# Agent attention and an MLP on one core: 128-row key subtiles, 512-token tiles, half as many native pairs, another queue order

## The chip, the core and the metric

The kernel runs on one core of a Trainium2 chip. The core has five engines with a queue each: TensorE (PE in the rows, with PEld its weight loads) makes matrix products into PSUM, VectorE (DVE), ScalarE (ACT) and GpSimd (POOL) work elementwise, and SyncE (SP) starts the transfers between HBM and SBUF. Each engine runs its own queue in order; semaphores make one wait for another. The metric is the device time in microseconds (us) of one execution; lower is better.

## What is computed

```python
def attn(q, k, v, agents):            # q, k, v [2, 12480, 128], agents [2, 49, 128]
    scale = 1.0 / np.sqrt(q.shape[-1])
    def sm(a, b):
        s = scale * (a @ b.transpose(0, 2, 1))
        e = np.exp(s - s.max(-1, keepdims=True))
        return e / (e.sum(-1, keepdims=True) + 1e-09)
    agent_v = sm(agents, k) @ v       # 49 agents look at all keys of their batch
    return sm(q, agents) @ agent_v    # each query looks at the 49 agents

def moe(x, w_in, w_out):              # x [24960, 128], w_in [128, 2048], w_out [2048, 128]
    h = x @ w_in
    g = np.where(h >= 1, h, np.where(h <= -1, 0.0, (h + 1) ** 2 / 4))
    return g @ w_out
```

The second function is applied to the result of the first, for all 2 x 12,480 tokens. The MLP's weights arrive as float64.

## The kernel before

The program has a start, in which the first batch's agent values are made, and a main loop over output tiles.

*Start.* The keys of batch 0 are loaded in 13 groups of 8 subtiles of 120 tokens (`kbuf`, four buffers, L419). For each subtile TensorE multiplies the keys, 120 columns of them as the stationary side, by the agents of both batches, 98 columns (`scores`, L442; a float32 product is two records of two passes each). ScalarE copies the scores to `ks`, VectorE keeps a running maximum, GpSimd subtracts it, and ScalarE takes the exponential. Then v is loaded in 13 groups of 8 subtiles (`vbuf`, four buffers, L542), and TensorE multiplies `ks` (stationary, 49 columns) by v with a column of ones beside it, 129 columns (`av`, L560). The ones give the softmax's sum. The sums of all groups (`acc`, L576), divided, are multiplied into w_in (`weights`, L624), so that the query's attention and the first MLP product become one product per tile. w_in and w_out are put together from their float64 words by VectorE and GpSimd (`decode`, L314 to L349).

*Main loop.* 52 tiles of 480 tokens. For each, `queries` scores four subtiles of 120 queries against the 49 agents (L660), takes a softmax (L673 to L708: maximum, difference, exponential, sum, an addition of 1e-9 at L692, reciprocal, product, and a split into a rounded high part and a rest), transposes it (L716) and copies it to `mt`, 98 rows of high and low parts. `pair` then takes 256 of the 2,048 hidden columns at a time, eight pairs a tile: four products into a PSUM pair `ph` (L755, w_hi and w_lo for two chunks; three such pairs exist), two ScalarE steps (`relu` L764, `square` L769) and a VectorE step (`gate` L772, which frees `ph`) that make g, then a high part `ghi` (`hi`, on VectorE L259 or ScalarE L257) and a low part `glo` (`lo` L783, on GpSimd or VectorE), and six products into the tile's accumulator bank (L793: ghi with w_out's high and low parts, glo with its high part). I call these six and the four ahead of them split products. In a native pair (N in `HI_ENG`) ghi and glo are left out and two float32 products take g as it is, four records of two passes each. `output` copies the bank (`ot`) and stores it.

*Batch 1's keys and values* go through the same steps during the main loop, with scores of 49 columns (the group's 120 rows by one batch's agents) in a free accumulator bank. Two of its key groups (16 subtiles) stand ahead of the first MLP product on TensorE.

*What sets the order.* `Order` (a planner inside the kernel) places each small operation by rough durations and by keys, the urgencies in `KEYS0`, `KEYS1`, `START` and `NEXT`; it fixes every engine's queue, and the order in which SyncE issues the transfers. Where `HI_ENG` or `LO_ENG` leaves a choice, it picks the engine too. The durations have no other effect.

## Time and profile before

| | |
|---|---|
| median of 3 runs | 1127.57 us (1126.28 to 1129.03) |
| the profiled execution: its span | 1129.6 us |
| TensorE busy | 1104.9 us, 98% |
| VectorE busy | 985.3 us, 87% |
| ScalarE busy | 961.0 us, 85% |
| GpSimd busy | 649.4 us, 57% |
| first MLP product begins | 86.6 us |
| transfers | 56.36 MB |

The profile is of one execution, and its span of 1129.6 us, from the first instruction to the last, is that execution's own time; it lies 2.0 us above the median. Busy time of TensorE counts products that overlap one another, so a full TensorE says little by itself; the distance from one product's start to the next one's tells what a product costs. The elementwise engines' records also reach some 0.1 us into the next one's.

### The profile page before, as it was taken

To read this page: it belongs to the slowest core of one execution; us is meant where nothing else is said; L and a number is where in the kernel's file an instruction comes from. 1 tells how busy PE (TensorE), PEld (TensorE's weight loads), DVE (VectorE), ACT (ScalarE), POOL (GpSimd) and SP (SyncE) were. 2 spreads that over 40 slices of the span, in tenths; PEclk is the share of its full clock that TensorE was granted. 3 is DMA by queue.
4 is the path that set the end of the run, shared out by engine and by line. 5 is a ranking of instruction groups with operands and counts; after the bars stand their busy time and mean duration, and the time that the engine had idled before them with its cause. 6 is when DMAs were issued, how large, how long until landed. Compare 5 with 4: busy or idle time off the path is not lost.

```text
span 1129.6 us, 15421 instructions
## 1 busy us (share of the span) xinstructions
PE 1104.9 (98%) x5546; PEld 919.5 (81%) x5546; DVE 985.3 (87%) x1310; ACT 961.0 (85%) x1155; POOL 649.4 (57%) x356
## 2 busy tenths in 40 slices
PE   9779999999999999999999999999999999999998
PEld 8657888888877888888887888888888888888886
DVE  7559998988897787888888999899999999999987
ACT  3219988989998888887898999999999999999997
POOL 2425756655676665555565565656565656565654
PEclk9889999999999999999999999999999999999999
DMA  8995111100002221200100101010101010100000
GB/s 302 205 257 121 53 53 38 51 18 27 20 25 53 62 62 45 62 18 18 36 19 20 34 18 35 18 36 19 36 18 35 18 36 18 36 10 18 10 18 18
DMA packets 47122, 56.36 MB, mean 50 GB/s; under 512 B 2758, under 2 KB 43334, under 8 KB 47046
## 3 DMA queue, kind: packets, MB, share of 16 engines
q1 hardware_dynamic: 47046, 55.37, 17.9%
q8 instruction: 44, 0.72, 0.3%
q14 instruction: 32, 0.26, 0.1%
HBM read 42.58 MB, written 12.78 MB: 49 GB/s over the span
## 4 chain that ended last, share of the span: by engine, by line
PE 91%; DMA 3%; ACT 2%; DVE 2%; SPq 1%; POOL 1%; issue 1%; DVEq 0%; ACTq 0%; POOLq 0%
PE bank L793 48%; PE ph L755 31%; PE bank L660 3%; PE bank L560 2%; PE ph L442 2%; PE bank L442 1%; PE bank L716 1%; DMA vbuf<-v_in 1%; ACT g L764 1%; DMA qt<-qT 1%; PE ph L560 1%; DVE g L772 1%; DMA kbuf<-kT 1%; POOL glo L783 1%; SPq L542 1%
## 5 line engine op out<-in xcount | busy, mean ns | idle before, releaser
L783 POOL TENSOR_TENSOR glo<-g,ghi 128x960 fp32r<-128x960 f32 x208 | 539.3, 2596 | 373.4 <-DVE ghi L259 298.5
L772 DVE SCALAR_TENSOR_TENSOR g<-g,ph 128x960 f32<-128x960 f32 x416 | 473.3, 1148 | 70.2 <-ACT g L769 39.4
L764 ACT ACTIVATE g<-ph,half 128x960 f32<-128x960 f32 x416 | 438.5, 1059 | 79.6 <-PE ph L755 56.9
L769 ACT ACTIVATE g<-g 128x960 f32<-128x960 f32 x416 | 414.4, 1004 | 5.2
L755 PE MATMUL ph<-mt,w_hi 98*128 98x480 f32 x832 | 334.7, 402 | 2.1 <-DVE g L772 2.1
L755 PE MATMUL ph<-mt,w_lo 98*128 98x480 f32 x832 | 315.1, 379 | 0.0
L793 PE MATMUL bank<-glo,wo_hi 128*128 128x480 f32 x728 | 225.0, 393 | 0.0
L793 PE MATMUL bank<-ghi,wo_hi 128*128 128x480 f32 x728 | 223.1, 387 | 0.9 <-ACT ghi L257 0.9
L793 PE MATMUL bank<-ghi,wo_lo 128*128 128x480 f32 x728 | 217.8, 380 | 0.0
L259 DVE CAST ghi<-g 128x960 fp32r<-128x960 f32 x312 | 207.0, 688 | 0.5
L783 DVE TENSOR_TENSOR glo<-g,ghi 128x960 fp32r<-128x960 f32 x156 | 183.3, 1180 | 6.4 <-ACT ghi L257 6.4
L755 PEld LDWEIGHTS ph<-mt,w_hi 98*128 98x128 f32 x832 | 156.4, 188 | 35.9 <-issue 5.5
L755 PEld LDWEIGHTS ph<-mt,w_lo 98*128 98x128 f32 x832 | 157.5, 189 | 30.6 <-issue 7.9
L793 PEld LDWEIGHTS bank<-glo,wo_hi 128*128 128x128 f32 x728 | 134.8, 189 | 26.5 <-issue 7.8
L793 PEld LDWEIGHTS bank<-ghi,wo_lo 128*128 128x128 f32 x728 | 136.6, 188 | 22.6
L793 PEld LDWEIGHTS bank<-ghi,wo_hi 128*128 128x128 f32 x728 | 133.0, 188 | 21.8 <-ACT ghi L257 1.3
L793 PE MATMUL bank<-g,wo 128*128 128x480 f32 x208 | 92.5, 567 | 0.0
L793 PEld LDWEIGHTS bank<-g,wo 128*128 128x128 f32 x208 | 39.0, 189 | 25.4 <-issue 22.6
L708 POOL TENSOR_TENSOR pq<-qd,pq 120x196 fp32r<-120x196 f32 x52 | 40.8, 786 | 26.3 <-ACT pq L257 26.3
L257 ACT ACTIVATE ghi<-g 128x960 fp32r<-128x960 f32 x52 | 52.0, 1000 | 2.3 <-DVE g L772 2.3
L660 PEld LDWEIGHTS bank<-ag,qt 128*120 128x120 f32 x392 | 48.7, 184 | 3.2
L698 POOL TENSOR_TENSOR qd<-qd,qsm 120x196 f32<-120x196 f32 x52 | 30.2, 582 | 30.7 <-DVE qsm L695 27.3
(88 smaller groups left out, 673.6 us busy)
## 6 DMA issues: line engine op xcount, KB each, us to landing
qt<-qT SPq DMA_DIRECT2D x52, 240.0 KB, 2.6
vbuf<-v_in SPq DMA_DIRECT2D x26, 480.0 KB, 8.3
outT<-ot SPq DMA_DIRECT2D x52, 240.0 KB, 2.0
kbuf<-kT SPq DMA_DIRECT2D x25, 480.0 KB, 5.4
raw<-w_in SPq DMA_DIRECT2D x4, 512.0 KB, 7.1
raw<-w_out SPq DMA_DIRECT2D x4, 512.0 KB, 10.6
kbuf<-kT SPq DMA_DIRECT2D x2, 240.0 KB, 3.4
ag<-agT SPq DMA_DIRECT2D x1, 49.0 KB, 2.3
```

Source lines behind the costliest of these rows:

```text
L257: act.activation(out=out, in_=in_, func=ACTF.Copy)
L259: dve.tensor_copy(out, in_)
L442: nc.tensor.matmul(out=dst, lhsT=kb[:, t * SUB:(t + 1) * SUB], rhs=rhs, start=True, stop=True,)
L560: nc.tensor.matmul(out=one(PS["v", b, g])[0:A, 0:C + 1], lhsT=ks[:, g * KG + t, :], rhs=vb[:, t, :], start=t == 0, stop=t == KG - 1,)
L660: nc.tensor.matmul(out=ps[0:SUB, i * A:(i + 1) * A], lhsT=st["q"][:, i * SUB:(i + 1) * SUB], rhs=ag[:, j // TPB, :], start=True, stop=True,)
L708: (pool if e == "POOL" else dve).tensor_tensor(out=st["pq"][:, :, A:A2], in0=st["d"], in1=st["pq"][:, :, 0:A].bitcast(F32), op=ALU.subtract,)
L755: nc.tensor.matmul(out=st["h"][:, c, 0:T], lhsT=w[:, f:f + 128], rhs=M[j], start=(n == 0), stop=(n == 1),)
L764: act.activation(out=st["g"], in_=st["h"][:, :, 0:T], func=ACTF.Relu, bias=half, scale=0.5)
L769: act.activation(out=st["g"], in_=st["g"], func=ACTF.Square)
L772: dve.scalar_tensor_tensor(out=st["g"], in0=st["g"], scalar=1.0, in1=st["h"][:, :, 0:T], op0=ALU.min, op1=ALU.max,)
L783: (pool if e == "POOL" else dve).tensor_tensor(out=st["lo"], in0=st["g"], in1=st["hi"].bitcast(F32), op=ALU.subtract)
L793: nc.tensor.matmul(out=bank[j % 2][:, 0:T], lhsT=w[:, f, :], rhs=x[:, c, :], start=first_mm, stop=LEFT[j] == 0,)
```

## The change

It touches sizes, layouts and the tables of the planner.

- Keys, v and the score buffers: subtiles of 128 tokens instead of 120, 7 in a group instead of 8, 14 groups a batch instead of 13; the last group is filled up with copies of the first keys and with zeros for v. The ones beside v come with the data, so that a group of v is one run of 3,612 bytes per partition in HBM and in SBUF instead of eight runs of 512 bytes.
- The scores of batch 0 take the 49 agents of one batch as the moving side, no longer 98.
- The agent-value product has 98 stationary columns: a subtile's 49 and the 49 that lie behind them, whose result isn't used (behind a group's last subtile lie zeros).
- w_out is laid out by partition on the host: a quarter is 4 KB per partition in one run instead of four of 1 KB.
- Tiles of 512 tokens: 48 whole ones and one of 384; the tile at the border of the batches does its first products in two parts (192 and 320 columns).
- `HI_ENG` has a native pair in every second tile (25 in all) instead of one in every tile (52), and leaves some choices to the planner.
- The addition of 1e-9 to the softmax's sum is gone; a column that holds 1e-9 beside `qd` is summed with the rest.
- New keys and durations for the planner, and so a new order of all queues.

```diff
-T = 480          # tokens per tile of the main loop
-SUB = 120        # tokens per partition tile
-NS = T // SUB    # subtiles per tile
...
+T = 512
+SUB = 128
+KG = 7
+HALF = 4
...
+HI_ENG = (("AD**DND*", "**DD*DDD",), ("*DDDAN*A", "DD**DDDA",))
+LO_ENG = (("DD***PPD", "*PP*DD*P",), ("P*D*DDDD", "DPDP*D*D",))
...
-START = dict(raw0=3.5, raw1=7.5, raw2=23.0, raw3=10.5, out0=55.5, out1=17.5, out2=103.5,
-             out3=61.5, q0=0.0, q1=19.1, q2=19.6, v=15.7, dec=171.0, dout=160.0, km=58.0,
-             qs0=90.0, qs1=109.5, qs2=100.0, sub=147.0, av=119.0, w=148.0, pm=40.0, split=7)
...
+START = dict(raw0=3.4, raw1=-28.1, raw2=23.4, raw3=26.2, out0=121.4, out1=83.7, out2=205.3,
+             out3=177.9, q0=-153.9, q1=115.1, q2=85.3, v=80.8, dec=140.8, dout=279.8, km=49.3,
+             qs0=152.0, qs1=313.4, qs2=-93.6, sub=34.5, av=65.1, w=29.3, pm=101.5, split=7)
...
-    ks = const.tile([SUB, NT, A], F32, name="ks")
...
+    ks = const.tile([SUB, NG, KG + 1, A], F32, name="ks")
+    ksf = ks.rearrange("p g t a -> p g (t a)")
...
+    qd = [const.tile([128, NSX, A + 1], F32, name=f"qd{i}") for i in range(BUFS["qs"])]
...
-        for vb in vbuf:
-            dve.memset(vb[:, :, C:C + 1], 1.0)
+        for d in qd:
+            dve.memset(d[:, :, A:A + 1], 1e-9)
+        pool.memset(ks[:, :, KG, :], 0.0)
...
-                    if on_bank:
-                        dst, rhs = ps[0:SUB, t * A:(t + 1) * A], ag[:, b, :]
-                    else:
-                        dst = ps[0:SUB, t // (KG // 2), t % (KG // 2) * A2:][:, 0:A2]
-                        rhs = ag.rearrange("c b a -> c (b a)")
                     nc.tensor.matmul(
-                        out=dst, lhsT=kb[:, t * SUB:(t + 1) * SUB], rhs=rhs,
-                        start=True, stop=True,
+                        out=ps[:, t * A:(t + 1) * A], lhsT=kb[:, t * SUB:(t + 1) * SUB],
+                        rhs=ag[:, b, :], start=True, stop=True,
                     )
...
-                nc.sync.dma_start(out=vb[:, :, 0:C], in_=v[b, :, g * KG:(g + 1) * KG, :])
-
-            LV[g] = load(SUB * KG * C * 4, fn, [first], v_key(g), ("v",))
+                nc.sync.dma_start(out=vb, in_=v[b, :, g * KG:(g + 1) * KG, :])
+
+            LV[g] = load(SUB * KG * (C + 1) * 4, fn, (), v_key(g), ("v",))
 
...
-                        out=one(PS["v", b, g])[0:A, 0:C + 1],
-                        lhsT=ks[:, g * KG + t, :],
+                        out=one(PS["v", b, g])[0:A2, 0:C + 1],
+                        lhsT=ksf[:, g, t * A:t * A + A2],
...
-            st["sm"] = small.tile([SUB, NS], F32, name="qsm", tag="qsm")
-            dve.tensor_reduce(out=st["sm"], in_=st["d"], axis=AX.X, op=ALU.add)
-
-        def eps(o, e):
-            dve.tensor_scalar(st["sm"], st["sm"], 1e-9, None, ALU.add)
+
+            st["sm"] = small.tile([128, NSX], F32, name="qsm", tag="qsm")[:, 0:ns]
+            dve.tensor_reduce(out=st["sm"], in_=full, axis=AX.X, op=ALU.add)
 
...
-                for n, w in enumerate(W[j // TPB]):
-                    nc.tensor.matmul(
-                        out=st["h"][:, c, 0:T], lhsT=w[:, f:f + 128], rhs=M[j],
-                        start=(n == 0), stop=(n == 1),
-                    )
+                for b, lo, hi in parts(j):
+                    for i, w in enumerate(W[b]):
+                        nc.tensor.matmul(
+                            out=st["h"][:, c, lo:hi], lhsT=w[:, f:f + 128], rhs=M[j][:, lo:hi],
+                            start=(i == 0), stop=(i == 1),
...
-            r = load_raw("out", wo_v[:, cs], n, h, PRO + START[f"out{2 * n + h}"], raw_in)
+            r = load_raw("out", w_out[:, cs], n, h, PRO + START[f"out{2 * n + h}"], raw_in)
...
-    NT = N // SUB
+    NT = -(-N // (SUB * KG)) * KG
+    token = np.arange(SUB * NT)
+    token[N:] -= N
+    vp = np.zeros((B, SUB * NT, C + 1), np.float32)
+    vp[:, 0:N, 0:C] = v
...
-        "v_in": np.ascontiguousarray(v.reshape(B, SUB, NT, C)),
...
+        "v_in": vp.reshape(B, SUB, NT, C + 1),
...
-        "w_out": np.ascontiguousarray(moe_w_out).view(np.uint64),
+        "w_out": np.ascontiguousarray(
+            moe_w_out.reshape(-1, 128, C).transpose(1, 0, 2)
+        ).view(np.uint64).reshape(128, -1),
```

TensorE's queue at the start, behind the seven products on `idle` that wake it: scores of batch 0's key groups (`kbuf`, one row a group), a query tile's scores (`qt`) and its transposes (`identr`). Before:

```order
L442 MATMUL ph<-ag,kbuf_110 120x98 x8
L660 MATMUL ph<-ag,qt 120x49 x4
L442 MATMUL ph<-ag,kbuf_111 120x98 x8
L442 MATMUL ph<-ag,kbuf_112 120x98 x8
L442 MATMUL ph<-ag,kbuf_113 120x98 x8
L716 MATMUL bank_91<-identr,pq 98x120 x4
L442 MATMUL ph<-ag,kbuf_110 120x98 x8
L442 MATMUL ph<-ag,kbuf_111 120x98 x8
L442 MATMUL ph<-ag,kbuf_112 120x98 x8
```

With the change:

```order
L472 MATMUL ph<-ag,kbuf_107 128x49 x7
L685 MATMUL ph<-ag,qt 128x49 x4
L472 MATMUL ph<-ag,kbuf_108 128x49 x7
L472 MATMUL ph<-ag,kbuf_109 128x49 x7
L472 MATMUL ph<-ag,kbuf_110 128x49 x7
L472 MATMUL ph<-ag,kbuf_107 128x49 x7
L472 MATMUL ph<-ag,kbuf_108 128x49 x7
L472 MATMUL ph<-ag,kbuf_109 128x49 x7
L472 MATMUL ph<-ag,kbuf_110 128x49 x7
```

The groups stand in the same order, with the result's columns 49 in place of 98 and seven subtiles in place of eight; the transposes come later. At the other end of the start, 21 subtiles of batch 1's scores stand ahead of the first MLP product now, 16 before.

SyncE's queue at the start, each row one transfer (`kbuf` keys, `qt` a query tile, `raw` a quarter of a weight, `ag` the agents). Before:

```order
L419 DMA kbuf_110<-kT 128x480
L399 DMA ag<-agT 128x98
L419 DMA kbuf_110<-kT 128x480
L655 DMA qt<-qT 128x480
L419 DMA kbuf_111<-kT 128x960
L419 DMA kbuf_112<-kT 128x960
L419 DMA kbuf_113<-kT 128x960
L372 DMA raw<-w_in 128x1024
```

With the change:

```order
L680 DMA qt<-qT 128x512
L404 DMA raw<-w_in 128x1024
L452 DMA kbuf_107<-kT 128x512
L432 DMA ag<-agT 128x98
L452 DMA kbuf_107<-kT 128x384
L452 DMA kbuf_108<-kT 128x896
L452 DMA kbuf_109<-kT 128x896
L452 DMA kbuf_110<-kT 128x896
```

A query tile and a quarter of w_in have moved ahead of the first keys.

ScalarE's queue in the second batch, far from any keys: `g<-ph` is relu, `g<-g` square, `ghi` a high part, and the other rows belong to query and output tiles. Before, 12 rows:

```order
L769 ACTIVATE g_8396<-g_8396 128x960
L764 ACTIVATE g_8414<-ph_8402,half_96 128x960
L769 ACTIVATE g_8414<-g_8414 128x960
L764 ACTIVATE g_8435<-ph_8422,half_96 128x960
L257 ACTIVATE ghi_8442<-g_8396 128x960
L769 ACTIVATE g_8435<-g_8435 128x960
L764 ACTIVATE g_8460<-ph_8444,half_96 128x960
L257 ACTIVATE mt_8470<-bank1_92 98x480
L769 ACTIVATE g_8460<-g_8460 128x960
L764 ACTIVATE g_8483<-ph_8462,half_96 128x960
L769 ACTIVATE g_8483<-g_8483 128x960
L764 ACTIVATE g_8505<-ph_8486,half_96 128x960
```

With the change:

```order
L788 ACTIVATE g_7669<-ph_7658,half_96 128x1024
L793 ACTIVATE g_7669<-g_7669 128x1024
L788 ACTIVATE g_7683<-ph_7673,half_96 128x1024
L285 ACTIVATE ghi_7696<-g_7643 128x1024
L793 ACTIVATE g_7683<-g_7683 128x1024
L788 ACTIVATE g_7708<-ph_7698,half_96 128x1024
L285 ACTIVATE ghi_7716<-g_7669 128x1024
L793 ACTIVATE g_7708<-g_7708 128x1024
L788 ACTIVATE g_7734<-ph_7711,half_96 128x1024
L788 ACTIVATE g_7739<-ph_7729,half_96 128x1024
L793 ACTIVATE g_7734<-g_7734 128x1024
L793 ACTIVATE g_7739<-g_7739 128x1024
```

High parts have come to ScalarE: by count 127 of 367 in the whole program, where there were 52 of 364, and in the second batch three in a tile with a native pair and two in one without. VectorE makes 240 where it made 312, and low parts are 158 on VectorE and 208 on GpSimd (156 and 208 before).

## Rows read from the trace of the kernel before

**Rows 1.** The page: its first line, TensorE's busy time, and the shares of the chain that ended last, by engine.

```profile
span 1129.6 us, 15421 instructions
...
PE 1104.9 (98%) x5546; PEld 919.5 (81%) x5546; DVE 985.3 (87%) x1310; ACT 961.0 (85%) x1155; POOL 649.4 (57%) x356
...
PE 91%; DMA 3%; ACT 2%; DVE 2%; SPq 1%; POOL 1%; issue 1%; DVEq 0%; ACTq 0%; POOLq 0%
```

**Rows 2.** The timeline of TensorE's products from 800 us, and of its weight loads (PEld). Columns: start us, time to the end of the last one us, engine, line, operation, written<-read, shape, count.

```profile
804.20 0.60 PE L793 MATMUL bank<-ghi,wo_hi 128*128 128x480 f32 x2
804.63 0.60 PE L793 MATMUL bank<-ghi,wo_lo 128*128 128x480 f32 x2
...
805.95 0.41 PE L716 MATMUL bank<-identr,pq 120*98 120x120 f32 x4
806.20 0.67 PE L793 MATMUL bank<-glo,wo_hi 128*128 128x480 f32 x2
...
808.46 0.94 PE L660 MATMUL bank<-ag,qt 128*120 128x49 f32 x8
809.22 0.47 PE L755 MATMUL ph<-mt,w_hi 98*128 98x480 f32 x1
809.53 0.38 PE L755 MATMUL ph<-mt,w_lo 98*128 98x480 f32 x1
...
801.68 0.19 PEld L793 LDWEIGHTS bank<-g,wo 128*128 128x128 f32 x1 [0.21 <-issue]
802.08 0.19 PEld L793 LDWEIGHTS bank<-g,wo 128*128 128x128 f32 x1 [0.21 <-issue]
```

**Rows 3.** The timeline of ScalarE in the second batch, with the same columns; from one output copy (`ot`) to the next.

```profile
965.36 0.57 ACT L257 ACTIVATE ot<-bank 128x480 f32<-128x480 f32 x1 [0.16 <-PE bank L793]
965.83 1.00 ACT L769 ACTIVATE g<-g 128x960 f32<-128x960 f32 x1
966.73 1.00 ACT L257 ACTIVATE ghi<-g 128x960 fp32r<-128x960 f32 x1
967.63 1.05 ACT L764 ACTIVATE g<-ph,half 128x960 f32<-128x960 f32 x1
968.57 0.36 ACT L257 ACTIVATE pq<-qd 120x196 fp32r<-120x196 f32 x1
968.83 1.00 ACT L769 ACTIVATE g<-g 128x960 f32<-128x960 f32 x1
...
977.53 0.56 ACT L257 ACTIVATE mt<-bank 98x480 fp32r<-98x480 f32 x1
977.98 1.01 ACT L769 ACTIVATE g<-g 128x960 f32<-128x960 f32 x1
...
984.29 0.57 ACT L257 ACTIVATE ot<-bank 128x480 f32<-128x480 f32 x1 [0.27 <-PE bank L793]
```

**Rows 4.** Busy time of each engine (us, with the number of instructions) in two stretches of the second batch; behind POOL the granted clock, the DMA share and GB/s.

```profile
600.00:850.00 250.00, 249.29 (x1178) 206.13 (x1177) 231.72 (x294) 231.82 (x275) 147.32 (x75) 1.00 0.08 26
850.00:1100.00 250.00, 250.00 (x1177) 207.69 (x1177) 232.80 (x289) 233.95 (x276) 147.24 (x73) 1.00 0.06 21
```

**Rows 5.** The timeline of TensorE's products in the start.

```profile
7.72 5.47 PE L442 MATMUL ph<-ag,kbuf 128*120 128x98 f32 x48
12.97 0.47 PE L716 MATMUL bank<-identr,pq 120*98 120x120 f32 x4
...
40.91 3.41 PE L660 MATMUL ph<-ag,qt 128*120 128x49 f32 x16 [3.62 <-DMA qt<-qT]
44.25 6.03 PE L560 MATMUL ph<-vbuf,ks 120*49 120x129 f32 x40
...
77.50 1.88 PE L442 MATMUL bank<-ag,kbuf 128*120 128x49 f32 x16
79.39 0.26 PE L604 MATMUL ph<-ident,av 49*128 49x49 f32 x1
...
86.60 0.79 PE L755 MATMUL ph<-mt,w_hi 98*128 98x480 f32 x1
```

**Rows 6.** Busy time by engine in stretches of the start, PE, PEld, DVE, ACT, POOL, then the granted clock of TensorE (1.00 is 2.4 GHz), the DMA share and GB/s.

```profile
6.30:30.00 23.70, 22.92 (x209) 22.06 (x208) 20.83 (x43) 8.91 (x19) 8.05 (x9) 1.00 0.97 320
...
40.40:44.20 3.80, 3.29 (x16) 3.27 (x16) 0.72 (x2) 0.65 (x2) 0.00 (x0) 0.50 1.14 200
44.30:47.10 2.80, 2.80 (x15) 2.68 (x15) 1.78 (x8) 0.82 (x3) 0.14 (x1) 0.50 1.05 217
47.30:60.70 13.40, 7.88 (x69) 7.17 (x68) 7.35 (x17) 2.20 (x5) 6.42 (x8) 1.00 1.10 204
...
77.50:81.20 3.70, 3.17 (x27) 2.96 (x27) 3.61 (x12) 0.50 (x1) 0.00 (x0) 1.00 1.05 392
81.40:84.60 3.20, 3.20 (x5) 1.16 (x4) 2.31 (x5) 0.74 (x2) 1.27 (x1) 0.50 0.99 247
```

**Rows 7.** VectorE's groups of instructions by line and shape: busy us, mean ns of one, idle time before them and what ended it.

```profile
L772 DVE SCALAR_TENSOR_TENSOR g<-g,ph 128x960 f32<-128x960 f32 x416 | 473.3, 1148 | 70.2 <-ACT g L769 39.4 <-issue 24.5 <-POOL glo L783 1.9
...
L259 DVE CAST ghi<-g 128x960 fp32r<-128x960 f32 x312 | 207.0, 688 | 0.5
L783 DVE TENSOR_TENSOR glo<-g,ghi 128x960 fp32r<-128x960 f32 x156 | 183.3, 1180 | 6.4 <-ACT ghi L257 6.4
...
L692 DVE TENSOR_SCALAR qsm<-qsm 120x4 f32<-120x4 f32 x52 | 42.2, 811 | 1.2
```

More of the change, by code (lines that the diff above doesn't have):

```diff
@@ L236, in agent_attention_moe, with width, parts, blocks @@
     wo_lo = const.tile([128, NC, 128], F32R, name="wo_lo")
+    def width(j):
+        return min(T, NTOK - j * T)
+    def parts(j):
+        t0, t1 = j * T, j * T + width(j)
+        return [
+            (b, max(t0, b * NB) - t0, min(t1, (b + 1) * NB) - t0)
+            for b in range(B) if t0 < (b + 1) * NB and t1 > b * NB
+        ]
+    def blocks(j):
+        return [
+            (i, b, max(lo - 128 * i, 0), min(hi - 128 * i, 128))
+            for b, lo, hi in parts(j)
+            for i in range(lo // 128, -(-hi // 128))
+        ]
+    def turn(j):
+        return parts(j)[0][0]
+    def plan(table, j):
+        turns = table[turn(j)]
+        return turns[j % len(turns)]
+    NSX = T // 128
     native = sorted({p for b in HI_ENG for e in b for p in range(NP) if e[p] == "N"})
-    def plan(table, j):
-        turns = table[j // TPB]
-        return turns[j % len(turns)]
     wo = {p: const.tile([128, 2, 128], F32, name=f"wo{p}") for p in native}
-    ks = const.tile([SUB, NT, A], F32, name="ks")
+    ks = const.tile([SUB, NG, KG + 1, A], F32, name="ks")
+    ksf = ks.rearrange("p g t a -> p g (t a)")
     gmax = const.tile([SUB, 2, A], F32, name="gmax")
@@ L925, in agent_attention_moe @@
         for p in range(NP):
[L926 removed]
+            pair(
+                j, p, [w_ops[b][2 * p // 4] for b, _, _ in parts(j)], wo_ops[2 * p // (NH // 2)]
+            )
         output(j)
```

268 lines of the change are left out of this document (136 added, 132 removed).

## The prediction

> **What bounds the kernel now.** I read the page first, then the start by stretches, then the matrix products one by one. TensorE is busy 98% of the span and 91% of the chain [rows 1]. A busy TensorE is not yet one at its peak, so I looked at spacings. In the main loop split products of 480 columns follow each other every 0.218 us (0.43 for two) without a gap, and a native (float32) pair is four records 0.40 us apart, 1.60 us [rows 2]. In the second batch an output tile takes 18.93 us (965.36 to 984.29 [rows 3]), and its products fill it: 74 x 0.218 + 1.60, transposes 0.25, query scores 0.85 (808.46 to 809.53 less one product [rows 2]) = 18.8 us. ScalarE is busy 93% there, GpSimd 59% [rows 4]. So the loop is bound by TensorE, and a change there is worth what it does to the sum of product times, as long as ScalarE and VectorE keep up.
>
> The start is different. The first MLP product runs at 86.60 us [rows 5], and TensorE's sum of products until then is only some 58 us at full clock. Keys and w_in arrive at 320 GB/s; while v is loaded the same queue, with its DMA share over 1.0, moves 200 to 217 GB/s [rows 6]; v goes in runs of 512 bytes, since the buffer's rows hold a 129th column (L542).
>
> **The clock in the start.** At 40.91 to 44.25 us TensorE made 16 records of 49-column query scores end to end, 0.209 us each, at half clock, and the clock stayed at 1.2 GHz until after 47.1, agent-value products having run since 44.25 [rows 5, 6]. From 77.50 to 81.20 it was busy 3.17 of 3.70 us, mostly with 49-column scores (0.118 us each), and the clock fell right after; between 47.3 and 60.7 it was busy only 7.88 of 13.40 us, but with products of 129 columns, and the clock held. The 98-column scores of 7.72 to 12.97 us ran at 0.109 us [rows 5], all under a full clock (6.3 to 30 [rows 6]). So the clock did not rise in one run of 49-column scores and fell after another, and it stayed up in the run of 98-column ones; the change turns that last run into 49-column scores. The Trainium skill, "TensorE: Matmul & The Clock Gate", "Part 1: The HAM clock gate", says that a busy TensorE releases the throttle. By that the score run of the change would be at full clock; rows 5 and 6, a full engine at 0.50, do not agree.
>
> **The change, part by part.**
>
> *MLP products.* Before: 3,848 split products x 0.218 = 838.9 us, 52 native pairs x 1.60 = 83.2; together 922.1. After: the columns are the same 24,960 tokens; 25 tiles have a native pair (12,672 tokens) and 24 none, so 3,802 split products over 1.921 million columns. The cost of 512 columns is not in the trace. Native passes run at 0.201 us per 480 columns (half of a 0.40 us record), 2.4 columns per ns; a split product of 480 costs 0.018 more, and a transpose of 120 columns 0.062 (four in 0.25 us [rows 2]), 0.012 over the 0.050 at that rate. The extra is thus about fixed, and I take 0.018 + columns/2.4: 68.4 + 800.3 = 868.7 us, and native 12,672 x 8 / 2.4 = 42.2. Together 910.9: **-11.2 us**. If it grew with width (0.233 at 512): 914.6, -7.5, the other end.
>
> *Keys, queries, agent values, transposes.* 416 score subtiles become 392, but of 128 rows instead of 120. A record took 0.109 with 98 result columns and no less, 0.118, with 49 [rows 5], so loading the rows sets it, and 392 x 128 is 416 x 120 within 1%: no change at full clock. Agent values: 208 subtiles x 4 passes x 129 columns / 2.4 = 44.7 us become 42.2 for 196; the stationary side grows from 49 to 98 columns, which a score record with its 120 does not show to cost over 0.109, about the 0.1075 of the product: nothing. Transposes: 208 of 120 columns become 195 of 128, -0.3. **-3 us** together (ends -1 and -4).
>
> *Elementwise engines.* From start to start, ScalarE needs 0.95 for a first step on g (relu), 0.90 for a square or ghi, 0.47 for ot, 0.45 for mt, 0.26 for pq and qd [rows 3]; by 0.90 at 960 and 0.26 at 196 elements, 64 more cost 0.054. A 512-token tile is 8 x (1.00 + 0.95) + 0.50 + 0.48 + 0.52 = 17.1 us, and to that come the ghi copies, 0.95 each: in the second batch three in a tile with a native pair and two in the other (one in each before). That makes 20.0 and 19.0 us, where TensorE needs 74 x 0.231 + 1.71 + 0.89 (scores of 128 rows) + 0.28 = 20.0 and 80 x 0.231 + 1.17 = 19.7. **ScalarE is left 0.3 us a tile**; before it was 17.2 of 18.93. VectorE gets lighter: per tile 8 x 1.148 + 6 x 0.688 + 3.3 x 1.180 + 0.811 = 18.0 of 18.93 [rows 7] become, scaled by 512/480, 8 x 1.225 + 5 x 0.734 + 4 x 1.259 = 18.5 of 19.85; the 52 small additions of 0.811 us that go free 42 us of an engine that isn't the bound: 0. For ScalarE's lack of slack nothing in the trace gives a price. From below it is 0 (TensorE still needs more). From above, ScalarE would idle as now, 34 of 500 us in rows 4, 1.3 us a tile: 20.8 us, +1.0 x 23.75 tiles = +24. I take **+4**, nearer to 0: a pair's second products stand about four pairs behind its first in either order, and 1.3 us of idle is what an engine with 1.7 to spare may have, not what it needs.
>
> *The start.* The first key stands behind 0.26 MB of q and 0.52 MB of w_in: scores from about 6 us. Fourteen groups are 196 records; at half clock 0.209 to 0.223 each, 41 to 44 us, plus a query and small things: keys done near 50.5. Four v loads are there by then. Two agent-value groups at half clock (129 columns x 2 passes / 1.2 = 0.215 a record; 15 of them fill 44.3 to 47.1 with 2.8 us [rows 6]) take 6, the other twelve 1.55 each (14 x 0.1075 and a little), queries 1.8: 77. The queue has the same to say: the fifth v waits for the first buffer, at 53.5, and from there ten v of 0.46 MB, half of w_out and two q are 6.2 MB, 21 us at 300 GB/s with rows now 3,612 bytes long, 2 for the landing: 76. Then 21 scores of the next batch (4.7), eight records of the first weights (3.4) and a landing: first MLP product near 86, as in [rows 5]. **0 us**, ends -5 and +5. v's rate is between 200 (no gain) and 320; I take 300, its rows being as long as those of keys. The Trainium skill, "DMA: Bandwidth & Descriptors", "Specifications", has 512 bytes as already enough for line rate; by that v gains nothing. Rows 6, with 200 against 320, do not agree.
>
> w_out in rows of 4 KB rides along in this; the ending tile of 384 tokens shortens the last chain by under 1 us; both sit in the ranges.
>
> **Sum.** The profiled execution's time is its span, 1129.6 us, 2.0 above the median of the runs. 1129.6 - 11.2 - 3 + 4 + 0 = 1119.4; against the median 1127.57 that is **1117.4 us**.
>
> **Rivals.**
> - *The score run keeps full clock.* For it: TensorE would be without gaps; against it: rows 5 and 6. Keys then end at the queue's pace, 8.9 MB at 300 near 31 us; all up to the last v, 17.4 MB, by 59; first MLP product near 70. -16: 1101. The Trainium skill's Part 1, above, gives this case.
> - *ScalarE becomes the bound in the second batch* (the other side). Place: tiles with a native pair, 20.0 us of ScalarE in 20.0 of TensorE. It outweighs all gains once ScalarE idles over 0.9 us a tile (0.3 slack, plus 14.2/23.75). At today's 1.3 us: 1127.6 - 14.2 + 24 = 1137. For it: hardly any slack; against it: the four pairs of distance.
> - *v loads gain nothing.* With half-clock keys the 6.2 MB take 31 us at 200: first MLP product near 96, +10: 1127, no change. The Trainium skill's line-rate figure, above, gives this case.
> - *The start worsens by more* (clock low for the agent values too, up to 8 us): 1125.
>
> **How the numbers follow.** Forecast (half-clock keys, ScalarE fits) 0.55, own range 1109 to 1124; full clock 0.20; ScalarE bound 0.12, of which 0.07 end above before; v without gain 0.05; worse start 0.08. A measurement of this kernel can tell about 0.2%, 1125.3 to 1129.8. Faster 0.84 (forecast, full clock, 0.03 of ScalarE, 0.06 of the start), slower 0.10 (0.07 ScalarE, 0.03 start and v), same 0.06. The range takes in the full clock and v without gain: 1098 to 1129.
>
> **What would show it.** In the new profile: granted clock 0.50 through the keys (about 6 to 50 us), scores 0.21 to 0.22 a record, v at 300 GB/s, first MLP product at 82 to 91 us; split products 0.231 apart; second-batch tiles averaging 19.9 to 20.1 us with ScalarE busy over 97%. Tiles of 20.5 us or more with idle before g1 on VectorE's gate would show ScalarE as bound; full clock at 20 us and a first product near 70 the other start. I am wrong most plainly if split products of 512 columns are spaced 0.24 or more, which alone takes 33 us.

## The result, and the profile after

The changed kernel takes 1139.26 us (median of 4 runs, 1136.10 to 1144.11) against 1127.41 (1126.28 to 1129.03) of the kernel before beside it: 1.0105 times as long, 95% interval 1.0075 to 1.0135. It is slower by 1%; 1117.4 was forecast. Its profiled execution took 1140.72 us, with a span of 1138.7.

The page of after, its first line, TensorE's busy time and the chain's shares by engine, which answer to [rows 1]:

```profile
span 1138.7 us, 14822 instructions
...
PE 1111.2 (98%) x5307; PEld 904.4 (79%) x5307; DVE 966.9 (85%) x1160; ACT 1004.2 (88%) x1169; POOL 657.7 (58%) x353
...
PE 72%; ACT 12%; DVE 8%; issue 4%; DMA 2%; POOL 1%; SPq 0%; DVEq 0%; ACTq 0%; POOLq 0%
```

TensorE's 98% stands as before, and says nothing. The chain tells more: 12% of it now runs over ScalarE and 8% over VectorE, where there were 2% each.

The busy times by stretch of after (PE, PEld, DVE, ACT, POOL, granted clock, DMA share, GB/s), for [rows 4, 6]; the third row is the first batch, and behind it stands the same stretch of the kernel before:

```profile
60.70:79.70 19.00, 17.52 (x159) 17.22 (x158) 10.44 (x28) 4.78 (x11) 9.55 (x11) 1.00 0.93 312
84.60:91.30 6.70, 6.70 (x14) 3.57 (x15) 5.26 (x9) 2.08 (x4) 1.93 (x3) 0.50 0.92 297
100.00:600.00 500.00, 484.13 (x2323) 389.79 (x2322) 431.58 (x482) 456.44 (x526) 341.66 (x174) 0.99 0.13 40
600.00:850.00 250.00, 249.47 (x1173) 200.75 (x1172) 221.72 (x261) 240.46 (x273) 138.94 (x71) 1.00 0.08 26
850.00:1100.00 250.00, 250.00 (x1132) 199.80 (x1131) 227.65 (x259) 247.73 (x281) 128.06 (x67) 1.00 0.06 22
```

```profile
100.00:600.00 500.00, 498.46 (x2510) 413.92 (x2509) 435.82 (x567) 439.03 (x521) 303.53 (x166) 1.00 0.13 38
```

Between 100 and 600 us TensorE idles 15.9 us after, 1.5 before. From 600 on it is full in both.

TensorE's products in the start of after and from 799 us (answers to [rows 2, 5]; columns: start us, time to the end of the last one, engine, line, operation, written<-read, shape, count, idle before and its releaser):

```profile
82.28 1.73 PE L472 MATMUL bank<-ag,kbuf 128*128 128x49 f32 x14 [1.55 <-DMA kbuf<-kT]
...
84.56 1.94 PE L472 MATMUL bank<-ag,kbuf 128*128 128x49 f32 x8 [0.36 <-ACT ks L285]
86.31 5.29 PE L645 MATMUL ph<-win,avT 128*98 128x512 f32 x6
91.44 0.77 PE L472 MATMUL bank<-ag,kbuf 128*128 128x49 f32 x6
92.04 1.06 PE L645 MATMUL ph<-win,avT 128*98 128x512 f32 x2
92.94 1.66 PE L472 MATMUL bank<-ag,kbuf 128*128 128x49 f32 x14
94.42 0.48 PE L781 MATMUL ph<-mt,w_hi 98*128 98x512 f32 x1
```

```profile
799.62 0.39 PE L781 MATMUL ph<-mt,w_lo 98*128 98x512 f32 x1
799.85 0.39 PE L781 MATMUL ph<-mt,w_hi 98*128 98x512 f32 x1
800.08 0.40 PE L781 MATMUL ph<-mt,w_lo 98*128 98x512 f32 x1
```

The first MLP product comes at 94.42 us, 7.8 later than before; split products of 512 columns follow each other every 0.23 us.

An account of the spans, 1129.6 to 1138.7, works as follows. I add the products of each kernel at their undisturbed spacings, and call lost what a stretch lasts beyond that. The sum falls from 1079.8 to 1065.8 us: -14.0. First MLP product: +7.8. Lost between 100 and 600 us: 10.5 before, 27.8 after, +17.3; of these 14.3 are the idle time of the rows above, the rest is half clock. What is left, -2.0, is the second batch and the end. The account is rough: the sums depend on the spacings taken, and the start's products stand in the first term and again in the second, so each term is good to about 2 us.

### The profile page after: what moved, and what is told of

It reads as the page before. It is cut to its first block, busy times and chain, and to the rows that moved or that the text cites. A ratio compares the mean times of both kernels' runs of the same rounds, so it can differ in the third digit from the quotient of the medians.

```text
span 1138.7 us, 14822 instructions
## 1 busy us (share of the span) xinstructions
PE 1111.2 (98%) x5307; PEld 904.4 (79%) x5307; DVE 966.9 (85%) x1160; ACT 1004.2 (88%) x1169; POOL 657.7 (58%) x353
## 4 chain that ended last, share of the span: by engine, by line
PE 72%; ACT 12%; DVE 8%; issue 4%; DMA 2%; POOL 1%; SPq 0%; DVEq 0%; ACTq 0%; POOLq 0%
PE bank L817 35%; PE ph L781 25%; ACT g L788 6%; DVE g L796 4%; ACT g L793 4%; PE ph L472 4%; PE bank L685 3%; DVE glo L807 2%; ACT ghi L285 1%; PE bank L581 1%; PE ph L581 1%; PE bank L472 1%; DVE ghi L287 1%; PE bank L738 1%; PE ph L645 1%
## 5 line engine op out<-in xcount | busy, mean ns | idle before, releaser
L807 POOL TENSOR_TENSOR glo<-g,ghi 128x1024 fp32r<-128x1024 f32 x208 | 544.3, 2624 | 298.3 <-DVE ghi L287 214.3
L796 DVE SCALAR_TENSOR_TENSOR g<-g,ph 128x1024 f32<-128x1024 f32 (+1 forms) x392 | 467.9, 1208 | 95.4 <-ACT g L793 54.0
L788 ACT ACTIVATE g<-ph,half 128x1024 f32<-128x1024 f32 (+1 forms) x392 | 429.8, 1112 | 24.5 <-PE ph L781 17.4
L793 ACT ACTIVATE g<-g 128x1024 f32<-128x1024 f32 (+1 forms) x392 | 408.8, 1061 | 2.5
L781 PE MATMUL ph<-mt,w_hi 98*128 98x512 f32 (+3 forms) x800 | 327.1, 410 | 14.5 <-DVE g L796 14.4
L781 PE MATMUL ph<-mt,w_lo 98*128 98x512 f32 (+3 forms) x800 | 312.8, 392 | 0.0
L817 PE MATMUL bank<-ghi,wo_hi 128*128 128x512 f32 (+1 forms) x734 | 232.0, 397 | 0.9 <-ACT ks L285 0.5
L817 PE MATMUL bank<-glo,wo_hi 128*128 128x512 f32 (+1 forms) x734 | 231.6, 398 | 0.2
L817 PE MATMUL bank<-ghi,wo_lo 128*128 128x512 f32 (+1 forms) x734 | 228.4, 392 | 0.0
L807 DVE TENSOR_TENSOR glo<-g,ghi 128x1024 fp32r<-128x1024 f32 (+1 forms) x159 | 221.0, 1399 | 2.4 <-ACT ghi L285 2.4
L781 PEld LDWEIGHTS ph<-mt,w_hi 98*128 98x128 f32 x800 | 151.2, 189 | 57.9 <-DVE g L796 17.5
L781 PEld LDWEIGHTS ph<-mt,w_lo 98*128 98x128 f32 x800 | 152.0, 190 | 35.5 <-issue 5.3
```

The costliest lines, as they stand in the source:

```text
L781: nc.tensor.matmul(out=st["h"][:, c, lo:hi], lhsT=w[:, f:f + 128], rhs=M[j][:, lo:hi], start=(i == 0), stop=(i == 1),)
L788: act.activation(out=st["g"], in_=st["h"][:, :, 0:n], func=ACTF.Relu, bias=half, scale=0.5)
L793: act.activation(out=st["g"], in_=st["g"], func=ACTF.Square)
L796: dve.scalar_tensor_tensor(out=st["g"], in0=st["g"], scalar=1.0, in1=st["h"][:, :, 0:n], op0=ALU.min, op1=ALU.max,)
L807: (pool if e == "POOL" else dve).tensor_tensor(out=st["lo"], in0=st["g"], in1=st["hi"].bitcast(F32), op=ALU.subtract)
L817: nc.tensor.matmul(out=bank[j % 2][:, 0:n], lhsT=w[:, f, :], rhs=x[:, c, :], start=first_mm, stop=LEFT[j] == 0,)
```

## The first batch: what TensorE waits for

The waits in the first batch of after, 108 to 620 us (engine, line, waited for: us in total, times, longest), and behind them VectorE's groups there (written<-read, shapes, count | busy us, mean ns of one | idle before them and its releasers):

```profile
PEld ph L781 <- DVE g L796: 15.5, 14, 2.4
PE ph L781 <- DVE g L796: 13.6, 12, 1.9
```

```profile
L796 DVE SCALAR_TENSOR_TENSOR g<-g,ph 128x1024 f32<-128x1024 f32 x184 | 220.1, 1213 | 56.7 <-ACT g L793 37.1 <-issue 10.0 <-POOL glo L807 8.5
L807 DVE TENSOR_TENSOR glo<-g,ghi 128x1024 fp32r<-128x1024 f32 x57 | 95.0, 1689 | 1.9 <-ACT ghi L285 1.9
L287 DVE CAST ghi<-g 128x1024 fp32r<-128x1024 f32 x108 | 90.5, 857 | 0.9
L492 DVE TENSOR_TENSOR pm<-pm,gmax 128x49 f32<-128x49 f32 x11 | 11.3, 1024 | 0.0
```

TensorE waits for the gate, which frees the accumulator of the next first product. The gate itself lasts what it should (1148 ns at 960 elements [rows 7], 1213 at 1024), but a low part takes 1689 ns on average where [rows 7] scaled gave 1259, and a running maximum of 49 columns takes 1024 ns. So something holds VectorE inside its instructions. The one long wait of TensorE at 336 us shows it. The timeline of after, VectorE, GpSimd and TensorE from 327 us (L781 is TensorE's first product, L796 the gate):

```profile
327.32 2.70 POOL L807 TENSOR_TENSOR glo<-g,ghi 128x1024 fp32r<-128x1024 f32 x1 [4.24 <-DVE ghi L287]
...
329.78 0.79 DVE L287 CAST ghi<-g 128x1024 fp32r<-128x1024 f32 x1
...
330.50 4.56 DVE L807 TENSOR_TENSOR glo<-g,ghi 128x1024 fp32r<-128x1024 f32 x2
...
330.72 3.25 POOL L807 TENSOR_TENSOR glo<-g,ghi 128x1024 fp32r<-128x1024 f32 x1 [0.70 <-DVE ghi L287]
...
334.98 2.34 DVE L796 SCALAR_TENSOR_TENSOR g<-g,ph 128x1024 f32<-128x1024 f32 x2
...
336.24 0.50 PE L781 MATMUL ph<-mt,w_hi 98*128 98x512 f32 x1 [1.95 <-DVE g L796]
```

VectorE begins two low parts at 330.50; together they take 4.56 us instead of 2 x 1.2. GpSimd begins one at 330.72 and ends at 333.97. The first VectorE operation ends at 331.7, the second one at 335.06, which is GpSimd's end and 1.1 us, its own time. The two engines share a port into SBUF, and each waits inside its instruction while the other has it: GpSimd until 331.7, then VectorE until 333.97. Behind VectorE's second low part stand the gates; they come 2.2 us late, and TensorE idles 1.95. Its clock then falls to 1.2 GHz from 337.1 to 343.9 us:

```profile
337.10:343.90 6.80, 6.80 (x24) 5.61 (x23) 4.50 (x7) 4.33 (x7) 4.76 (x3) 0.50 0.14 39
```

The planner knows of the port: it gives one operation at a time to it. Its plan at this place has both of VectorE's low parts first and GpSimd's behind them. On the chip GpSimd's operation needs only its high part; that was there at 330.6, so it stood at the port while VectorE made its first low part, and got it before the second. I call this an inversion. In 90 to 600 us 43 VectorE operations of after are stretched by over 0.3 us, 55.1 us in all, and each of them ends its own duration, within 0.15 us, after a GpSimd operation ends. Of the 17 that are stretched by over 1.5 us ten are low parts, four running maxima, two high parts and one a `pq`; behind 11 of the 17 VectorE's next operation is a gate. In the kernel before they are 27 with 24.8 us, 17 of them the small addition on the query's sums (L692) that the change removed. The Trainium skill, "SBUF — State Buffer", "SBUF: two separate sides", says that a GpSimd operation and a VectorE operation with two inputs in SBUF or in a mode of two ports lock the shared ports: the one that starts first has them for its whole instruction, and the other blocks. These rows agree.

## Experiments

### The clock in the start: c98, before49

Theory: 49-column key scores keep TensorE at 1.2 GHz, and that delays the start. Rival: transfers or the order set it. c98 is the changed kernel with 98 result columns in batch 0 (and a copy out of PSUM in two halves, not shown):

```diff
-                ps = one(PS["k", b, g])
+                ps = PS["k", b, g]
                 for t in range(lo, hi):
+                    if on_bank:
+                        dst, rhs = ps[:, t * A:(t + 1) * A], ag[:, b, :]
+                    else:
+                        dst = ps[:, t // HALF, t % HALF * A2:][:, 0:A2]
+                        rhs = ag.rearrange("c b a -> c (b a)")
```

> The changed kernel, but the key scores of batch 0 are products of 98 columns (both batches' agents) again, the unused 49 left in PSUM, and the copy out of PSUM is in two halves. If the start loses to the clock (49-column scores hold it at 1.2 GHz): granted clock 1.00 through the keys, a score record 0.11 to 0.12 us instead of 0.213, keys done by 40 us instead of 51.6, first MLP product at 70 to 82 us instead of 94.4, time 1115 to 1127 us. If the start is set by the transfers or by the order: first MLP product within 4 us of 94.4 and time 1135 to 1143 us whatever the clock does.

before49 is the reverse in the kernel before (with the copy in one piece, not shown):

```diff
-                    if on_bank:
-                        dst, rhs = ps[0:SUB, t * A:(t + 1) * A], ag[:, b, :]
-                    else:
-                        dst = ps[0:SUB, t // (KG // 2), t % (KG // 2) * A2:][:, 0:A2]
-                        rhs = ag.rearrange("c b a -> c (b a)")
+                    dst, rhs = ps[0:SUB, t * A:(t + 1) * A], ag[:, b, :]
```

> The kernel before, with 49-column key scores in batch 0 and nothing else changed. If 49-column scores hold the clock at 1.2 GHz: clock 0.50 through the keys, a score record 0.20 to 0.22 us instead of 0.109, keys done near 52 us, first MLP product 6 to 16 us later than 86.6, time 1133 to 1144 us. If the clock would rise anyway, or the slower keys lie wholly beside the v loads: time 1125 to 1130 us.

Measured: c98 1124.0 us (1121.59 to 1127.57), 0.9957 of the kernel before (0.9938 to 0.9977); before49 1139.9 (1138.24 to 1142.68), 1.0110 (1.0083 to 1.0136). The first stretch of the keys, c98 ahead, then before49, after and b0_tables (a run of the next section, whose start is that of after), and TensorE's scores in after from 11.4 to 35.3 us and in c98 from 17 to 35 us (behind the bar: busy us, mean ns of one):

```profile
10.00:35.00 25.00, 23.62 (x179) 23.22 (x178) 17.82 (x41) 6.97 (x26) 4.71 (x6) 1.00 0.75 248
```

```profile
10.00:35.00 25.00, 25.00 (x129) 25.00 (x129) 12.95 (x28) 4.55 (x10) 2.29 (x4) 0.50 0.66 210
```

```profile
10.00:35.00 25.00, 25.00 (x119) 25.00 (x118) 12.57 (x28) 4.22 (x10) 2.60 (x3) 1.00 0.59 181
```

```profile
10.00:35.00 25.00, 25.00 (x121) 24.99 (x121) 12.39 (x28) 4.73 (x11) 2.59 (x3) 0.50 0.59 183
```

```profile
L472 PE MATMUL ph<-ag,kbuf 128*128 128x49 f32 x112 | 24.1, 413 | 0.0
```

```profile
L477 PE MATMUL ph<-ag,kbuf 128*128 128x98 f32 x140 | 16.6, 278 | 1.4 <-DMA kbuf<-kT 1.4
```

The 1.00 of after is no measurement: its trace has no clock record before 57.2 us, where the clock rises, and where there is none the rows print 1.00. What shows its clock is the spacing of its scores and b0_tables, with the same products in TensorE's queue through the start, whose record has 0.50 from 8.1 to 52.5 us. The record of c98 begins at 17.0 us, and its scores ahead of that are 0.213 us apart as well, so the rows of c98's scores begin there.

112 scores of after fill 24.1 us, 0.215 each (scores overlap, so the mean is longer than the spacing); 140 of c98 fill 16.6, 0.119 each, with twice the columns. Keys end at 38 us instead of 51.6, the first MLP product comes at 78.1 instead of 94.4, and 15 us are gained. Eleven are lost by the same edit backwards in the kernel before. With keys of 49 columns the clock stayed at 1.2 GHz to their end (in before49 from 8.6 us, in b0_tables from 8.1); with 98 it was at 2.4 in the kernel before, and in c98 it rose after 6 us of them. The theory stands in both directions, and the rival falls.

### The first batch's tables and urgencies: b0_tables, b0_keys

```diff
-HI_ENG = (("AD**DND*", "**DD*DDD",), ("*DDDAN*A", "DD**DDDA",))
-LO_ENG = (("DD***PPD", "*PP*DD*P",), ("P*D*DDDD", "DPDP*D*D",))
+HI_ENG = (("*DDDAN*A", "DD**DDDA",), ("*DDDAN*A", "DD**DDDA",))
+LO_ENG = (("P*D*DDDD", "DPDP*D*D",), ("P*D*DDDD", "DPDP*D*D",))
```

> The changed kernel, but batch 0 takes the HI_ENG and LO_ENG rows of batch 1, so that VectorE makes most of the low parts there and GpSimd fewer. If the first batch loses because VectorE waits for the port that it shares with GpSimd (uneven, up to six low parts of a tile on GpSimd): TensorE's lost time between 108 and 600 us falls from about 27 us to 17 or less, time 1126 to 1132 us. If it loses by the order that KEYS0 makes: lost time stays within 5 us, time 1134 to 1144 us. If batch 0's other work on GpSimd and ScalarE (keys of the next batch) is what makes its table different, then it is slower than 1144 us.

Measured 1155.8 us (1152.9 to 1157.66). The third case came: VectorE now has 86 low parts instead of 56 in 100 to 600 us, is busy 447.9 of 500 us, and GpSimd waits for it up to 12 us at a time. Fewer low parts on GpSimd is not the remedy; that VectorE has no room for them beside the next batch's keys is my reading of it.

b0_keys has the urgencies of the kernel before in the first batch:

```diff
-KEYS0 = dict(g1=-1.5, relu=2.1, square=-55.7, gate=16.5, hi=-7.7, lo=1.9, g2=5.0, g2l=6.7,
-             out=25.1, q=-9.6, qm=8.3, qe=9.2, qt=17.6, qn=10.0, qh=14.8, ql=14.6, tr=10.4,
-             mc=-49.9)
+KEYS0 = dict(g1=0.5, relu=5.0, square=1.9, gate=3.2, hi=1.2, lo=-0.1, g2=5.0, g2l=6.6,
+             out=12.1, q=-4.0, qm=-6.8, qe=0.7, qt=3.9, qn=8.8, qh=7.9, ql=1.5, tr=14.7,
+             mc=10.0)
```

> The changed kernel, with the urgencies KEYS0 of the kernel before. If the first batch loses by its order (operations issued too late or too early on VectorE and ScalarE): TensorE's lost time between 108 and 600 us falls by 8 us or more, time 1126 to 1132 us. If it loses to the shared port (the engine tables): the lost time stays within 5 us, time 1134 to 1144 us.

Measured 1139.8 us (1137.95 to 1143.91). The loss in 100 to 600 us fell to 22, VectorE's stretched time to 24.4 us; but 10.7 us were lost between 600 and 800, against 2.0 in after. Neither case came whole (the loss fell by under 8 us, but by more than 5). That is inconclusive: a list of urgencies changes the whole queue, and no such edit tells a cause apart. What was needed was one that leaves the order alone.

### The inversions themselves: c98_wait, c98_half, after_wait, before_wait

c98_wait keeps every queue of c98 as it is and adds only waits: where the planner put a VectorE operation ahead of a GpSimd one at the port, GpSimd waits for it. (`o.port` is the planner's note that the operation takes the port; `made` lists the instructions of an engine.)

```diff
+        before = None
         for o in ops:
+            n = len(pool.made)
             o.fn(o, o.engine)
+            if o.port and o.engine == "DVE":
+                before = dve.made[-1]
+            elif o.port:
+                if before is not None:
+                    tc.add_manual_dep(
+                        pool.made[n].ins, before.ins.name,
+                        mybir.DependencyInfo(
+                            mybir.DependencyClass.Sync, mybir.DependencyReason.DATA
+                        ),
+                        reason="port",
+                    )
+                before = None
```

> c98 (1124 us) with the same order on every engine, but each GpSimd operation that takes the shared port also waits for the VectorE operation that the planner put ahead of it at the port. In c98, 44 VectorE operations between 90 and 600 us lasted 55.6 us longer than alone, each until a GpSimd operation ended that had begun ahead of its planned place. If these inversions at the port make the first batch's loss: the VectorE low parts fall from 1.63 us to under 1.35 us, TensorE's lost time in 100 to 600 us from 23 us to under 12, time 1108 to 1117 us. If the waits only cover other idle time of VectorE, or GpSimd becomes late instead: lost time stays over 18 us, time 1121 to 1132 us.

Measured 1099.5 us (1095.68 to 1100.70), 0.9754 (0.9726 to 0.9782): more than expected. VectorE's low parts and high parts in 108 to 620 us, and the stretch of the first batch, in c98_wait (L94 is the wrapper that notes each VectorE and GpSimd instruction):

```profile
L94 DVE CAST ghi<-g 128x1024 fp32r<-128x1024 f32 x115 | 100.6, 894 | 1.1
L94 DVE TENSOR_TENSOR glo<-g,ghi 128x1024 fp32r<-128x1024 f32 x60 | 78.3, 1326 | 0.8 <-ACT ghi L296 0.8
```

```profile
100.00:600.00 500.00, 500.00 (x2448) 407.90 (x2447) 424.21 (x501) 475.50 (x548) 319.86 (x178) 1.00 0.12 38
```

TensorE does not idle at all there, and no half clock is left between 86 us and the end; the loss in 100 to 600 us is 2.8 instead of 23.1. GpSimd waits for VectorE's low parts 43 us in exchange, and VectorE's gates wait for GpSimd no longer than in c98 (5.0 us in 108 to 620, there 8.5). VectorE is still stretched by 29.5 us, mostly in high parts. So the port's total of waiting is not the loss; what costs is a wait that the plan does not have, ahead of gates. Of the gain over c98, 4.5 us lie ahead of the loop: the first MLP product comes at 73.6 instead of 78.1, with the clock at 2.4 GHz there (in c98 it fell at 68.2). In after_wait, below, the same waits gain nothing there, so I don't put that part down to the port.

c98_half halves the suspected wait instead: each low part on GpSimd in two instructions.

```diff
+            if e == "POOL":
+                for c in range(2):
+                    pool.tensor_tensor(
+                        out=st["lo"][:, c], in0=st["g"][:, c],
+                        in1=st["hi"][:, c].bitcast(F32), op=ALU.subtract,
+                    )
+                return
```

> c98 with every low part on GpSimd made in two halves (one per chunk), order otherwise as it is. If VectorE's loss is the wait for a whole GpSimd operation at the port: the wait of one VectorE operation falls from up to 2.2 us to about 1.2, the sum of such waits in 90 to 600 us from 55 us to 20 to 35, TensorE's lost time there by 6 us or more, time 1112 to 1120 us. If the loss has another cause: time 1122 to 1130 us (212 more GpSimd instructions at about 0.1 us).

Measured 1112.9 us (1111.05 to 1115.59). The first batch in c98, then in c98_half:

```profile
100.00:600.00 500.00, 485.80 (x2340) 392.00 (x2339) 429.14 (x478) 458.88 (x528) 341.18 (x175) 0.99 0.12 37
```

```profile
100.00:600.00 500.00, 494.54 (x2398) 399.39 (x2397) 423.11 (x488) 469.16 (x541) 373.81 (x294) 1.00 0.12 38
```

No VectorE operation is stretched by over 1.5 us any more (the longest wait is 1.2 instead of 2.2), their sum is 39.9 us, TensorE idles 5.5 us instead of 14.2, and the loss in 100 to 600 us is 11.2 instead of 23.1. With each wait about halved, about half the loss is gone.

after_wait is the changed kernel, 49-column keys and all, with the waits of c98_wait alone.

> The changed kernel (1139.3 us, 49-column keys kept) with only the wait of c98_wait added: a GpSimd operation that takes the shared port waits for the VectorE operation planned ahead of it. If the inversions at the port and the clock in the start are two separate losses that add up: the main loop gains what it gained from c98 to c98_wait, 24 us, first MLP product still at 92 to 97 us, time 1112 to 1118 us. If the first batch's loss is a consequence of the late start: time 1130 us or more.

before_wait is the kernel before with them.

> The kernel before with the same wait added. Its VectorE operations stretched at the port sum to 24.8 us in 90 to 600 us (55.6 in c98), 19 of 27 of them the small additions of the query chain, and TensorE lost 10.5 us between 100 and 600 us. If that loss too is inversion at the port: time 1118 to 1123 us. If the stretched operations of before are ones that nothing waits for: within 3 us of the kernel before. If GpSimd becomes late by the wait: slower by more than 3 us.

Measured: after_wait 1114.2 us (1112.54 to 1116.28), 0.9866 (0.9820 to 0.9913), first MLP product at 95.4 us, in the range named. This is the cleanest of the four: the same queues as in after, nearly the same start, and 25 us less. At the place of the timeline above GpSimd's low part now begins at 321.60, behind the end of VectorE's second one (321.46), which takes 1.21 us instead of 3.42. The start's loss and the inversions are two losses that add up. before_wait 1126.7 us (1123.26 to 1135.13), 0.9993 (0.9965 to 1.0021): no difference. The first batch in after_wait, and in before_wait VectorE's group that stands for most of its stretched time:

```profile
100.00:600.00 500.00, 498.97 (x2446) 406.96 (x2445) 424.63 (x502) 478.37 (x552) 319.82 (x181) 1.00 0.13 41
```

```profile
L94 DVE TENSOR_SCALAR qsm<-qsm 120x4 f32<-120x4 f32 x24 | 17.6, 734 | 0.6
```

The second case of the expectation came. But the waits took little of the stretched time away: counted alike in both, 27 us before and 24 in before_wait, the additions 1095 ns long before and 734 with the waits. So most of it is where the plan too has GpSimd ahead, and nothing on TensorE's path hangs on it. Which part of the change moved them in front of gates, the new order or the addition that is gone, was not told apart.

### The next batch's first keys: c98_b1

Ahead of the first MLP product stand 49-column scores of the next batch, and in c98 the clock fell behind them at 68 us. c98_b1 gives the first three groups 98 columns, each product overwriting the unused half of the one before.

```diff
+                    if on_bank and g < 3:
+                        dst = ps[:, t * A:t * A + A2]
+                        rhs = ag[:, b:b + 2, :].rearrange("c b a -> c (b a)")
+                    elif on_bank:
```

> c98 with 98-column products also for the first three groups of the next batch's key scores (66 to 80 us), each overwriting the unused half of the one before; same order. If the run of 49-column scores is what makes the clock fall at 68 us: no stretch of 0.50 between 60 and 78 us, the six products of the first weights in 2.7 us instead of 5.2, first MLP product at 74.5 to 76.5 us instead of 78.1, time 1119 to 1123 us. If the waits for the last keys (1.5 us of idle at 64.5) make it fall: the clock falls as before, time 1122 to 1126 us.

Measured 1123.0 us (1119.75 to 1129.55), 0.9959 (0.9934 to 0.9985), c98's 0.9957. From 66 to 76 us, c98 ahead, then c98_b1:

```profile
66.00:76.00 10.00, 9.64 (x36) 6.16 (x37) 6.80 (x15) 3.23 (x7) 3.18 (x3) 0.66 0.81 288
```

```profile
66.00:76.00 10.00, 9.23 (x54) 6.72 (x55) 9.42 (x21) 4.86 (x10) 5.74 (x4) 1.00 0.94 332
```

The clock stays up there and the first MLP product comes at 75.4 instead of 78.1. But the clock falls at 83.4 and stays low until 90.2, where c98 had a fall of half that length; the gain is given back. It is no proof either: with 49 columns c98_wait kept its clock until 83.0, and c98_vold below until 85.3. What decides in this stretch stays open.

### Why v is faster now: c98_vold, vold_120, vold_wout

I had put v's 200 GB/s [rows 6] down to runs of 512 bytes. c98_vold loads such runs again (the column of ones is set once, not shown):

```diff
-                nc.sync.dma_start(out=vb, in_=v[b, :, g * KG:(g + 1) * KG, :])
+                nc.sync.dma_start(
+                    out=vb[:, :, 0:C], in_=v[b, :, g * KG:(g + 1) * KG, 0:C]
+                )
```

> c98 with v loaded as before (runs of 512 bytes into a buffer with a 129th column that is set once), the rest as it is. If the long rows of v are what lifts the queue from 200 to over 300 GB/s: 200 to 220 GB/s while v is loaded, first MLP product at 85 to 93 us instead of 78.1, time 1131 to 1139 us. If the layout is indifferent: over 290 GB/s, first product within 2 us of 78.1, time 1121 to 1127 us.

Measured 1123.8 us (1121.86 to 1130.96), 0.9973 (0.9952 to 0.9993), first MLP product at 76.4. For the time the row length is indifferent, though from 50 to 60 us the queue moved 287 GB/s, 327 in c98. Two more differences of the kernel before were then put back into c98_vold one at a time: transfers of 120 partitions,

```diff
+                for p in (slice(0, 120), slice(120, SUB)):
                     nc.sync.dma_start(
-                    out=vb[:, :, 0:C], in_=v[b, :, g * KG:(g + 1) * KG, 0:C]
+                        out=vb[p, :, 0:C], in_=v[b, p, g * KG:(g + 1) * KG, 0:C]
                     )
```

> c98_vold (v in runs of 512 bytes, 128 partitions, 287 to 303 GB/s) with each load of v cut into one of 120 partitions and one of 8. If 120 partitions instead of 128 are what held v at 200 GB/s in the kernel before: 200 to 230 GB/s in 40 to 60 us, a 512-byte packet 45 ns or more instead of 27 (median), first MLP product 4 to 12 us later than 76.4. If not: over 280 GB/s, first product within 3 us.

and w_out in rows of 1,024 bytes (its array as in the kernel before).

> c98_vold with w_out in its layout of before (packets of 1,024 bytes instead of 4,096), which came between the v loads there. If the mixture of v with the short rows of w_out is what held the queue at 200 GB/s: 200 to 240 GB/s where the two are loaded together, first MLP product 3 to 10 us later than 76.4. If not: over 270 GB/s there, first product within 3 us.

Measured: vold_120 1137.2 us (1132.04 to 1138.34), first MLP product at 90.2; vold_wout 1123.6 (1122.13 to 1127.27), at 78.4. From 40 to 50 us in c98_vold, vold_120 and vold_wout:

```profile
40.00:50.00 10.00, 9.21 (x77) 8.45 (x75) 4.15 (x15) 3.92 (x10) 5.97 (x8) 1.00 1.08 297
```

```profile
40.00:50.00 10.00, 7.77 (x63) 6.93 (x62) 4.70 (x14) 3.70 (x10) 5.52 (x8) 1.00 1.12 220
```

```profile
40.00:50.00 10.00, 9.60 (x83) 9.07 (x82) 5.48 (x19) 4.45 (x14) 6.13 (x8) 1.00 1.09 292
```

The DMA engines are busy in all three (share over 1.0), but from 40 to 60 us with 120 partitions a 512-byte packet takes 45 ns instead of 27 (median), about the time it took in the kernel before (46). It is not v's packets alone: those of 2,048 bytes take 138 ns instead of 88, those of 4,096 bytes 235 instead of 159. vold_120 also has two transfers for one; the kernel before has the slow packets with one transfer of 120 partitions each, so it isn't the number of transfers. It is thus the 128-row subtiles, for the most part, that lifted v to 300 GB/s, and not the 129th column in its rows. The Trainium skill, "DMA: Bandwidth & Descriptors", "Why a DMA increments its semaphore by 16 and not by 1", says that a transfer uses the largest number of engines up to 16 that divides its outermost dimension; that would make 15 for 120 partitions and 16 for 128. By that the loss would be one sixteenth; 297 against 220 GB/s is more, so the rule is at most a part. Why a packet itself takes longer stays open.

## Why the prediction was wrong, step by step

- **MLP products: right.** 0.231 us for 512 columns was the estimate, 0.23 is the spacing from 799.62 us; with transposes and agent values -14.0 came of the 14.2 forecast (good to about 2 us).
- **The clock in the keys: right,** 0.215 us a score, keys done at 51.6 us against 50.5 forecast. The sign that I had named, 0.50 in the profile of after, is not to be had there, since the record begins later; b0_tables has it. One reading was too kind: the clock that "held" from 47.3 to 60.7 us fell right behind that, at 60.8, for 3.4 us. The other case (1101 us, 0.20) did not come. The rule behind it, the Trainium skill's "TensorE: Matmul & The Clock Gate", "Part 1: The HAM clock gate", does not agree with before49's row either: 25.00 of 25.00 us busy at 0.50.
- **v at 300 GB/s: right in size** (312), by luck, for the reason was wrong: partitions, not row length, for the most part. The line rate at 512 bytes in the Trainium skill, "DMA: Bandwidth & Descriptors", "Specifications", which I set aside, agrees in the main with c98_vold's 297 GB/s.
- **The start, 0 us with ends of -5 and +5: mis-sized, +7.8.** Agent values ended at 79.9 instead of 77; keys for the next scores were 1.55 us late; and the term "eight records of the first weights (3.4)" was priced at one clock for all, where six of them took 5.29 us at 1.2 GHz, as [rows 6] had shown for the same place before (0.50 at 81.4); the eight cost some 2.5 us more than forecast. The larger fault lies under it: the forecast held the start equal and so missed that c98's start was to be had, 16 us earlier.
- **ScalarE in the second batch, +4: nothing.** Output copies stand at 867.88, 891.23 and 907.77 us, 39.9 for two tiles, 19.95 each where 19.9 to 20.1 were named; ScalarE is busy 247.73 of 250 us. TensorE idles 0.5 in 500. The rival that made ScalarE the bound (1137) ends near the measured time, and is still wrong: 0 us of it.
- **VectorE, "gets lighter: 0": the step that failed.** Priced as a sum of durations, it has 1.35 us a tile to spare. The sum was near (227.65 of 250 us busy in the second batch, 18.2 a tile), and beside the point: what counts is which operation stands at the port ahead of a gate. [Rows 7] held the hint, small additions of 811 ns on a tile of four columns, most of it waiting (the shortest took 0.16 us). I took their removal for idle time that goes free, and did not ask who would stand at the port in their place. And the second batch, which I read closely, is not where the next batch's keys are made; I had no row of the first batch. The runs put this term at +25 us of time (after to after_wait), of which +17 show against the loss of the kernel before. That after_wait's 1114 us lies near the 1117 forecast is partly luck: a start 8.8 us later is set off by ScalarE's +4 that did not come and by less loss in the first batch than the kernel before has.
- **The other side.** The forecast gave 0.10 to slower, by ScalarE or the start. The start took its part, +7.8; but what made the kernel slower is a mechanism that I had not listed.

With both losses away, c98_wait takes 1099.5 us, 2.5% under the kernel before: about -14 in products, -13 at the first MLP product (73.6 us), -8 of loss in 100 to 600 us, of 35.7 us between the profiled spans (1129.6 and 1093.9). It beats both kernels.
